# Attention, MoE and gated MLP on one core: weight pieces, x loads and output buffers in the last stage rearranged

## The chip, the cores and the metric

The kernel runs on one core of one Trainium2 chip. The metric is the device time of one execution in microseconds (us), the median of several; lower is better. Every number in this document comes from these times or from the profile of one execution, unless it says otherwise. TensorE is PE in the profile's rows, VectorE DVE, ScalarE ACT, SyncE SP; "SPq" and "ACTq" are the instructions with which SP and ScalarE issue DMAs.

## The reference

Three stages follow one another, in fp32; the two weight-heavy ones, cut to what matters:

```python
S, D, E, F = 576, 512, 8, 1024
attn = softmax(q @ k.T / sqrt(64) + mlp(relative log positions)) @ v
x = attn.transpose(0, 2, 1, 3).reshape(2304, 512)

e_idx = argmax(x @ w_gate, axis=1)
for e in range(8):
    h = maximum(x[mask_e] @ w1[e], 0)
    out[mask_e] = gate * sigmoid_gate * (h @ w2[e])

g = x @ w_gate2
y = (g * sigmoid(g) * (x @ w_val)) @ w_out
```

q, k and v are (4, 8, 576, 64). In the last stage w_gate2 and w_val are (512, 1536) and w_out is (1536, 512); these three lie in DRAM as 64-bit floats, while everything is computed in 32 bits.

## The kernel before

Every fp32 product is made of three products of a high and a low part (hi and lo). A hi part is a ScalarE copy into the matmul type, a lo part a VectorE subtraction of that copy from the value. So each weight that TensorE uses has passed one ScalarE and one VectorE instruction of its own. VectorE and ScalarE work strictly in the order of the program, and so does SP's queue, which issues nearly all DMAs: an instruction that waits holds back what stands behind it.

**Stages.** Attention runs until about 305 us of the span. Then come 64 MoE steps (`h_step`, `y_step`, L582 to L600; 4 batches, 2 halves of the tokens, 8 pieces of the expert), each with 24 products. For each batch one expert is done for all tokens; the tokens of other experts are left to 8 `q_h`/`q_y` steps for one rest expert (L699, L713) and, where these do not do, to a loop (`loop`, L1167). Work beside the steps is hung on step numbers in a list `todo` (`at(n, f)`): after the products of step n, the entries of n are put in the program. Tables such as NS, QL and EC at the top of the file say which step gets what.

**Weight pieces of the last stage.** w_gate2, w_val and w_out are cut into 12 pieces each, 36 in all, numbered 3f + i (f the piece, i which matrix). A piece is 128 x 512 values of 64 bits, 512 KB. `fetch_w` (L969) loads one and `narrow_w` (L977) makes 32-bit floats of it with one ScalarE instruction (`expo`, L984) and three VectorE ones (`b1`, `b2`, `b3`, L987 to L993), where b1 works in place in the raw piece and must not start before `expo` has read it. The hi and lo parts follow (`w_hi`, L1004; `w_lo`, L1007). Three kinds are told apart:

- pieces 0 to 5 ("early", `early_ld`, `early_cv`) are loaded and converted in late MoE steps and kept on chip;
- pieces 6 to 3*NPL - 1, with NPL = 7, are converted during the first NPL steps of the last stage, three in a step (`n_tasks`, L1386), from two raw buffers (`n_load`, L1381): when a piece has been converted, the piece two further on is asked for;
- the 15 pieces from 3*NPL on ("stash", L1016) are converted in the MoE steps of the table NS and written to a DRAM tile `wn` as 32-bit values; later they are read back (`r_load`, L1372).

Pieces of the first two kinds are stored in `wn` too, for use in the other token blocks.

**Last stage.** 36 steps: 3 blocks of 768 tokens (j), 12 pieces (f) each. Function `it(n)` (L1530) writes out step n. TensorE makes g in bank X and the value in bank Y for the two halves of a block, and, in between, the 18 output products of the step before (`outs`, L1503). The first NPL steps of block 0 are "plain": 48 products for X and Y, which need only the weight pieces. The others use sums of quarters of x and of the weights (S1 to S4, made by `x_add`, L1222; the weights' by `w_sums`) in a scheme of seven products (P1 to P7) instead of eight, which takes 42. S1 to S4 get hi and lo parts through `x_hi` (L1228) and `x_lo` (L1235). The extra work of a step is put at letters a to h between the products (`fills`, `x_fill`), and at one letter a VectorE instruction stands ahead of what the step itself needs. In a plain step VectorE's multiply `p_mul` (L1272) reads Y and releases it for the next Y product; there is one for each half, and each stands behind the extra work of its letter (b or f).

x for the sums is loaded by `ld_x` (L1449): for block 0 at the end of step 2 with eight DMAs, and for the next blocks a step after the 7-product steps began. At the end of a block's last step, called pair end here (the sums of the next block are split there, letters c to h of step 11), S1 goes at letter g and S4 at h, and A22 at c of the next step.

**Rest expert.** Its weights are loaded in three parts by `load_w` (L527, the DMAs L533 and L534) into two large rotating buffers of tag "vt", which the raw early pieces use as well (L1030). The table QL gives the steps of the three loads, QC the step of the first conversion (`conv_w`, L539, with L550 on ScalarE and L552 on VectorE).

**End.** In the last step the six output tiles leave through `ot`, three rotating buffers of 512 columns (L1514), copied from PSUM by VectorE (L1524) or ScalarE (L1526) and stored by SP or ScalarE (L1528, L1520, L1521).

Of the kernel before, what the change touches and what calls it, by code (L numbers as in the profile page):

```python
# [37 lines left out]
N0, NPL = 6, 7  # L38
NS = (9, 10, 11, 18, 19, 20, 21, 24, 25, 26, 34, 35, 38, 40, 41)
# [6 lines left out]
QL, QC = ((55, 54, 60), 58)  # L46
# [66 lines left out]
def body(tc, qt, kt, va, vb, ws, moe_w_gate, moe_w_output_gate, moe_w1, moe_w2, w_gate, w_val, w_out, ctab, cst, cst2, out):  # L113
    nc = tc.nc
    with ExitStack() as ctx:
# [900 lines left out]
        def stash(i, n, m):  # L1016

            def cv():
                for f in narrow_w(s_raw(i), s_out(i)):
                    f()  # L1020
                nc.sync.dma_start(wn[n], s_out(i))
            at(m, cv)
# [4 lines left out]
        early = {}  # L1027
# [6 lines left out]
        def early_cv(n):  # L1034
            i, o = divmod(n, 2)
            fs = []
            t = lambda: early[i][:, 2048 + 512 * o:2560 + 512 * o].bitcast(F32)

            def expo():
                if o == 0:  # L1040
                    early["w"] = pers.tile([128, NTOK], F32R, tag=f"xT{i}", name="w0")
                w = early["w"]
                wt.setdefault(n // 3, {})[n % 3] = w[:, 1024 * o:1024 * o + 512], w[:, 1024 * o + 512:1024 * o + 1024]
                fs.extend(narrow_w(early[i][:, 1024 * o:1024 * o + 1024], t()))
                fs[0]()

            def bits():
                for f in fs[1:]:
                    f()
                nc.sync.dma_start(wn[n], t())  # L1050
# [14 lines left out]
        todo = {}  # L1065
# [21 lines left out]
        for i, m in enumerate(NS):  # L1087
            stash(i, 3 * NPL + i, m)
# [61 lines left out]
        for n in range(16 * B):  # L1150
# [12 lines left out]
            if n:  # L1163
                for f in todo.get(n, []):
                    f()
# [190 lines left out]
        with ExitStack() as c2:  # L1356
# [15 lines left out]
            def r_load(f):  # L1372
                if f % 2:
# [59 lines left out]
            def fills(n):  # L1433
# [5 lines left out]
                if 2 <= f < NPL:  # L1439
                    ts = [n_tasks(3 * f + i) for i in range(3)]  # L1440
                    for k, i, js in (("a", 0, (0,)), ("b", 0, (1, 2, 3)), ("c", 0, (4,)), ("c", 1, (0, 1)), ("c", 0, (5,)), ("d", 1, (2, 3)), ("e", 1, (4,)), ("e", 2, (0, 1)), ("e", 1, (5,)),
# [7 lines left out]
            def ld_x(j):  # L1449
                t = xq["xr"] = wp.tile([128, 3072], F32, tag="xr", name="xr").rearrange("p (k h n) -> p k h n", k=4, h=2)  # L1450
                for k in range(4):
                    def row(a, o, w, b, c):
                        nc.sync.dma_start(t[:, k, :, o:o + w], x2[k, :, b, c:c + 2 * w].rearrange("p o (h n) -> p (o h) n", h=2))  # L1453
                    if j == 0:
                        row(0, 0, 256, bass.ds(r0, 1), 0)
                        row(0, 256, 128, bass.ds(r1, 1), 0)
                    elif j == 1:
                        row(0, 0, 128, bass.ds(r1, 1), 256)
                        row(0, 128, 256, bass.ds(r2, 1), 0)
                    else:  # L1460
                        row(0, 128, 256, slice(3, 4), 0)
# [7 lines left out]
            def x_fill(j, i):  # L1469
# [9 lines left out]
                if j and i == 0:  # L1479
                    d["c"] = [lambda: xq["hi"]("A22"), lambda: xq["lo"]("A22")]  # L1480
# [3 lines left out]
                if i == NF - 1 and j < 2:  # L1484
                    for k, v in zip("cdefgh", ("A11", "A12", "S2", "S3", "S1", "S4")):
# [17 lines left out]
            def outs(n, h, m):  # L1503
# [9 lines left out]
                if last:  # L1513
                    o = wp.tile([128, DM], F32, tag="ot", bufs=3, name="ot")  # L1514
                    end = j == 2
                    parts = rows(j, h, m)
# [13 lines left out]
            def it(n):  # L1530
# [19 lines left out]
                if n == N:  # L1550
                    c2_mul(p, nc.vector)
# [81 lines left out]
            n_load(6)  # L1633
            n_load(7)
# [23 lines left out]
```

## Time and profile before

| what | value |
|---|---|
| median of 3 runs | 996.12 us (993.75 to 1000.24) |
| the profiled execution | 996.18 us |
| its span in the trace | 994.3 us |
| its mean granted TensorE clock | 0.991 |
| TensorE busy | 957.6 us, 96% |
| VectorE busy | 690.8 us, 69% |
| ScalarE busy | 528.9 us, 53% |
| share of the chain that ended last | TensorE 35%, VectorE 4%, ScalarE 2%, DMA 2% |

The span is the time from the first to the last event of the trace; the 1.9 us between it and the execution's time lie around it. Busy time leaves out register, branch and semaphore work. The granted clock is what the throttle let TensorE have, as a share of full speed. A bracket behind a row, as [2.06 <-DVE c L1272], is the idle time of that engine ahead of the row and the instruction that ended it. The chain of the last row is a walk back from the last instruction, at each step to what released it.

### The profile page before, as it was taken

The page shows a single profiled execution, that of the slowest core. Times are in us where ns is not written, and L with a number is a line of the kernel's source. Part 1 is how long each engine was busy: PE and PEld are TensorE (multiplying, and loading weights), DVE is VectorE, ACT ScalarE, POOL GpSimd, SP SyncE. Part 2 cuts the span into 40 slices and gives each one's busy share as a digit, 9 for nine tenths or more (in the row PEclk, how much of TensorE's full clock was granted, in tenths as well). Part 3 has the DMA queues.
Part 4 walks back from the last instruction along what each step waited for, and adds up shares of the span by engine and source line. Part 5 has one row for each costly group of instructions (what it writes and reads, how often), then busy time and mean ns, then how long its engine had stood idle before and what let it go on. Part 6 is the DMA issues. An engine that isn't in the chain of part 4 may idle for free. (4 is left out here: it accounts for less than half of the span.)

```text
span 994.3 us, 19678 instructions
## 1 busy us (share of the span) xinstructions
PE 957.6 (96%) x7639; PEld 816.4 (82%) x7639; DVE 690.8 (69%) x1540; ACT 528.9 (53%) x1121; POOL 115.7 (12%) x116
## 2 busy tenths in 40 slices
PE   7979999999999999999998998999999999999997
PEld 2347777777668999999997897899899998999996
DVE  8977788777787477666555566877646677456663
ACT  6777777777775253433434443454534445335542
POOL 2673333343310000000000000000000000000000
PEclk9999999999999999999999999999999999999999
DMA  6785324333044564936745566440122420311111
GB/s 202 206 257 164 117 82 150 96 119 112 2 135 147 172 224 148 343 124 226 237 140 175 169 198 207 145 142 1 53 75 64 127 64 1 128 32 64 64 32 64
DMA packets 88383, 129.47 MB, mean 130 GB/s; under 512 B 13760, under 2 KB 46528, under 8 KB 88288
## 3 DMA queue, kind: packets, MB, share of 16 engines
q1 hardware_dynamic: 87664, 127.28, 39.9%
q8 instruction: 60, 0.98, 0.4%
q10 hardware_dynamic: 624, 0.92, 0.3%
q14 instruction: 35, 0.29, 0.1%
HBM read 92.71 MB, written 35.46 MB: 129 GB/s over the span
## 5 line engine op out<-in xcount | busy, mean ns | idle before, releaser
L271 DVE CUSTOM_DVE_ANT_0 E<-S,bias 128x576 f32<-128x576 f32 x128 | 91.8, 755 | 32.4 <-PE S L267 25.9
L276 ACT ACTIVATE E<-E,st 128x576 f32<-128x576 f32 x144 | 110.4, 769 | 4.3 <-DVE st L271 3.9
L1256 PE MATMUL Y<-fv,ws 128*128 128x384 f32 x522 | 105.4, 336 | 0.2
L1256 PEld LDWEIGHTS Y<-fv,ws 128*128 128x128 f32 x522 | 92.4, 188 | 3.8 <-DVE c L1281 0.7
L267 PEld LDWEIGHTS S<-kh,qz 64*128 64x128 f32 (+1 forms) x576 | 57.7, 189 | 38.5 <-DVE st L271 21.0
L378 PE MATMUL pv<-pt,rawv 128*64 128x320 f32 (+1 forms) x576 | 88.1, 422 | 0.0
L267 PE MATMUL S<-kh,qz 64*128 64x288 f32 (+1 forms) x576 | 84.0, 325 | 3.9 <-DVE st L271 2.6
L1512 PE MATMUL o<-ws,u 128*128 128x512 f32 x306 | 84.5, 395 | 1.2 <-DVE u L1311 1.2
L591 ACT ACTIVATE qz<-T 128x288 fp32r<-128x288 f32 x63 | 25.8, 409 | 89.5 <-PE T L589 89.3
L317 ACT ACTIVATE pt<-T 128x512 f32<-128x512 f32 (+3 forms) x112 | 50.7, 468 | 40.4 <-PE T L294 40.0
L1256 PE MATMUL X<-fr,ws 128*128 128x384 f32 x348 | 70.9, 338 | 0.0
L1007 DVE TENSOR_TENSOR ws<-r,ws 128x512 fp32r<-128x512 f32 (+1 forms) x63 | 49.1, 779 | 30.3 <-ACT ws L1004 29.5
L1256 PEld LDWEIGHTS X<-fr,ws 128*128 128x128 f32 x348 | 62.8, 188 | 5.5
L1512 PEld LDWEIGHTS o<-ws,u 128*128 128x128 f32 x306 | 56.2, 188 | 8.7 <-DVE u L1311 2.5
L602 PE MATMUL y<-qz,w2hl 128*128 128x288 f32 x384 | 57.0, 296 | 2.1 <-DVE qz L592 0.8
L319 DVE COPY pt<-T 128x512 f32<-128x512 f32 (+3 forms) x112 | 55.8, 522 | 3.3 <-PE T L294 3.1
L592 DVE SCALAR_TENSOR_TENSOR qz<-T,qz 128x288 fp32r<-128x288 f32 x63 | 28.7, 455 | 41.4 <-ACT qz L591 40.8
L589 PE MATMUL T<-xh,whl 128*128 128x288 f32 x256 | 56.9, 298 | 0.0
L602 PE MATMUL y<-qz,whl 128*128 128x288 f32 x384 | 56.7, 296 | 0.1
L589 PE MATMUL T<-xh,w1hl 128*128 128x288 f32 x248 | 55.7, 300 | 0.0
L602 PEld LDWEIGHTS y<-qz,w2hl 128*128 128x128 f32 x384 | 52.7, 188 | 3.5 <-ACT qz L591 2.3
L294 PE MATMUL T<-ident,E 64*128 64x64 f32 x1248 | 55.3, 224 | 0.0
(308 smaller groups left out, 2136.7 us busy)
## 6 DMA issues: line engine op xcount, KB each, us to landing
raww<-in_moe_w_dram SPq DMA_DIRECT2D x16, 768.0 KB, 6.7
r<-wn SPq DMA_DIRECT2D x21, 512.0 KB, 3.6
bscr<-ob SPq DMA_DIRECT2D x36, 288.0 KB, 3.6
bias<-bscr SPq DMA_DIRECT2D x14, 576.0 KB, 4.3
ro<-wn SPq DMA_DIRECT2D x21, 256.0 KB, 2.8
rawq<-in_qt_dram SPq DMA_DIRECT2D x16, 320.0 KB, 3.6
rawk<-in_kt_dram SPq DMA_DIRECT2D x16, 288.0 KB, 3.2
x<-xT SPq DMA_DIRECT2D x16, 288.0 KB, 6.3
```

What stands on the lines that cost most here:

```text
L267: nc.tensor.matmul(t[:, f, 0:288], x[k, a], y[k, o], start=i == 0, stop=i == 2)
L271: nc.vector.tensor_tensor_reduce(out=E.rearrange("p (a b) -> p a b", a=2), in0=ps[:, :, 0:288], in1=bt[p, hh, c].rearrange("p (a b) -> p a ...
L276: nc.scalar.activation(E, E, AF.Exp, bias=st[:, 2 * c + hh:2 * c + hh + 1], scale=-1.0, accum_out=st[:, 10 + 2 * c + hh:11 + 2 * c + hh])
L294: nc.tensor.transpose(t[r][:, at:at + 64], E[k, o:o + 128], ident[k, k])
L317: nc.scalar.activation(o, x, AF.Copy)
L319: nc.vector.tensor_copy(o, x)
L378: nc.tensor.matmul(st["ps"][64 * hh:64 * hh + 64, 0:w], vt[p][:, hh, b, c, :], y, start=c == order[0], stop=c == order[4])
L589: nc.tensor.matmul(ps, wa[:, x, k], xs[k][y][:, o], start=k == 0 and i == 0, stop=k == 3 and i == 2)
L602: nc.tensor.matmul(hbuf["y"][d // 2][:, d % 2, 0:288], wb[:, x, d], t[:, y:y + 288], start=f == 0 and i == 0, stop=(one or f == 7) and i == 2)
L1007: return lambda: eng.tensor_tensor(l, t, h.bitcast(F32), ALU.subtract)
L1256: nc.tensor.matmul(bank, a[:, c], x[:, k], start=first and k == 0 and n == 0, stop=k == 1 and n == 2, skip_group_check=True)
L1512: nc.tensor.matmul(t, u, w, start=first and i == 0, stop=last and i == 2)
```

## The change

It has seven parts, and the line numbers of the changed file lie 1 to 21 higher.

1. NPL goes from 7 to 6. One plain step becomes a 7-product step, and its three pieces (18 to 20) join the stash: NS has 18 entries at partly other steps, and four of them (NS2) leave the last instruction of the conversion to the next step.
2. The stores of stashed and early pieces into `wn` are hung on a second list `done` (`after(n, f)`), whose entries come behind all of `todo` in a step, and one to two steps later than before.
3. The rest expert's loads move from steps 55, 54, 60 to 58, 55, 61 (QL).
4. Raw pieces are fetched three ahead instead of two: every third takes a tile of the tag r0. In the plain steps the exponent of a piece (`expo`) is put ahead of the hi part of the piece before it.
5. x for the blocks 0 and 1 is loaded with four DMAs instead of eight, and for block 2 with ten instead of twelve. With NPL = 6, S1 and S2 are made in step 3 and S3 and S4 in step 4 (before 4 and 5), while the load stays at the end of step 2.
6. At the pair ends S1 moves from letter g to h, S4 from h to c of the next step, and A22 from c to d there.
7. The last step's output goes through one tile `oend` of six slices in the place of x (tag xr).

The diff, cut to its core:

```diff
-N0, NPL = 6, 7
-NS = (9, 10, 11, 18, 19, 20, 21, 24, 25, 26, 34, 35, 38, 40, 41)
+N0, NPL = 6, 6
+NS = (9, 10, 13, 18, 19, 20, 21, 24, 25, 26, 29, 34, 35, 37, 39, 40, 41, 43)
+NS2 = (13, 29, 37, 43)
-QL, QC = ((55, 54, 60), 58)
+QL, QC = ((58, 55, 61), 58)
-        def stash(i, n, m):
+        def stash(i, n, m, two):
...
-                for f in narrow_w(s_raw(i), s_out(i)):
-                    f()
-                nc.sync.dma_start(wn[n], s_out(i))
-            at(m, cv)
+            at(m, lambda: cv(0, 4 if not two else 3))
+            if two:
+                at(m + 1, lambda: cv(3, 4))
+            after(m + 1 + two, lambda: nc.sync.dma_start(wn[n], s_out(i)))
...
+            after((52, 52, 54, 54, 57, 57)[n], lambda: nc.sync.dma_start(wn[n], t()))
...
-                for f in todo.get(n, []):
+                for f in todo.get(n, []) + done.get(n, []):
                     f()
...
-                    nw[n] = wp.tile([128, 1024], I32, tag="nraw", bufs=2, name="nraw")
+                    if n % 3 < 2:
+                        nw[n] = wp.tile([128, 1024], I32, tag="nraw", bufs=2, name="nraw")
+                    else:
+                        nw[n] = wp.tile([128, 2048], F32, tag="r0", name="nr2").bitcast(I32)[:, 0:1024]
...
-                    n_load(n + 2)
+                    n_load(n + 3)
...
+                def row(o, w, b, c):
+                    for h in range(2):
+                        nc.sync.dma_start(t[:, :, h, o:o + w], x2[:, :, b, c + h * w:c + h * w + w].rearrange("k p o n -> p k (o n)"))
+                if j == 0:
+                    row(0, 256, bass.ds(r0, 1), 0)
+                    row(256, 128, bass.ds(r1, 1), 0)
...
                 if j and i == 0:
-                    d["c"] = [lambda: xq["hi"]("A22"), lambda: xq["lo"]("A22")]
+                    for k, v in zip("cd", ("S4", "A22")):
+                        d[k] = [lambda v=v: xq["hi"](v), lambda v=v: xq["lo"](v)]
...
-                    for k, v in zip("cdefgh", ("A11", "A12", "S2", "S3", "S1", "S4")):
+                    for k, v in zip("cdefh", ("A11", "A12", "S2", "S3", "S1")):
...
-                    o = wp.tile([128, DM], F32, tag="ot", bufs=3, name="ot")
                     end = j == 2
+                    if end:
+                        o = sv["end"][:, 512 * (3 * h + m):512 * (3 * h + m) + 512]
+                    else:
+                        o = wp.tile([128, DM], F32, tag="ot", bufs=3, name="ot")
```

**Where instructions move: SP's queue at the end of the MoE.** The names: raww are the rest expert's weights, rw0 the raw early pieces with their 32-bit values, qz00 a tile of x. Before:

```order
L533 DMA raww_7322<-in_moe_w1_dram 128x4x384
L534 ISA
L534 DMA raww_7322<-in_moe_w2_dram 128x3x512
L759 ISA
L759 DMA qz00_114<-x2_120 128x4x256
L533 ISA
L533 DMA raww_7360<-in_moe_w1_dram 128x4x384
L534 ISA
L534 DMA raww_7360<-in_moe_w2_dram 128x3x512
L1050 DMA wn_4870<-rw0_7252 128x512 x2
L533 ISA
L533 DMA raww_7542<-in_moe_w1_dram 128x4x256
```

And of the change:

```order
L760 DMA qz00_114<-x2_120 128x4x256
L534 ISA
L534 DMA raww_7375<-in_moe_w1_dram 128x4x384
L535 ISA
L535 DMA raww_7375<-in_moe_w2_dram 128x3x512
L1067 DMA wn_4870<-rw0_7270 128x512 x2
L534 ISA
L534 DMA raww_7492<-in_moe_w1_dram 128x4x384
L535 ISA
L535 DMA raww_7492<-in_moe_w2_dram 128x3x512
L534 ISA
L534 DMA raww_7593<-in_moe_w1_dram 128x4x256
```

The store of the last early pair stood behind the second request for raww and stands ahead of it now; that request takes another buffer than before (the program's numbers behind the names tell buffers' uses apart, not the buffers).

**ScalarE in the second plain step.** tw are 32-bit pieces, nraw and nr2 raw ones, ws the hi parts, c1 and c2 results from bank X. Before:

```order
L984 ACTIVATE tw_8098<-nraw_8089 128x512
L1268 ACTIVATE c1_8095<-X_8093 128x384
L1308 ACTIVATE u00_8085<-c1_8095 128x384
L1004 ACTIVATE ws_8097<-tw_8098 128x512
L984 ACTIVATE tw_8138<-nraw_8091 128x512
L1268 ACTIVATE c2_8096<-X_8093 128x384
L1004 ACTIVATE ws_8097<-tw_8138 128x512
L984 ACTIVATE tw_8170<-nraw_8117 128x512
L1308 ACTIVATE u10_8087<-c2_8096 128x384
L1004 ACTIVATE ws_8097<-tw_8170 128x512
```

And of the change:

```order
L985 ACTIVATE tw_8118<-nraw_8107 128x512
L1279 ACTIVATE c1_8115<-X_8113 128x384
L1319 ACTIVATE u00_8103<-c1_8115 128x384
L985 ACTIVATE tw_8157<-nraw_8109 128x512
L1005 ACTIVATE ws_8117<-tw_8118 128x512
L1279 ACTIVATE c2_8116<-X_8113 128x384
L985 ACTIVATE tw_8189<-nr2_8111 128x512
L1005 ACTIVATE ws_8117<-tw_8157 128x512
L1319 ACTIVATE u10_8105<-c2_8116 128x384
L1005 ACTIVATE ws_8117<-tw_8189 128x512
```

The exponent of the second piece (tw from nraw) stood behind the hi part of the first and now stands ahead of it, and likewise for the third, which comes from nr2.

**VectorE in the fourth plain step (step 3), of the change.** sx are the sums of x, xr is x, nraw a raw piece, Y the bank:

```order
L1008 TENSOR_TENSOR ws_8232<-tw_8301,ws_8232 128x512
L1322 TENSOR_TENSOR fv_7968<-c2_8231,fv_7967 128x384
L988 TENSOR_SCALAR nraw_8252<-nraw_8252 128x512
L991 SCALAR_TENSOR_TENSOR tw_8349<-tw_8349,nraw_8252 128x512
L994 SCALAR_TENSOR_TENSOR tw_8349<-nraw_8252,tw_8349 128x512
L1233 TENSOR_TENSOR sx_8342<-xr_8337 128x768
L1283 TENSOR_TENSOR c1_8345<-Y_8344,c1_8345 128x384
```

The sixth row is S1. In the same step of the kernel before nothing stands there: the multiply of Y and c1 comes right behind the three instructions of the piece, and S1 follows one step later.

## Rows read from the trace of the kernel before

**Rows 1.** Page part 1, whole span: busy time of each engine, share, instructions.

```profile
PE 957.6 (96%) x7639; PEld 816.4 (82%) x7639; DVE 690.8 (69%) x1540; ACT 528.9 (53%) x1121; POOL 115.7 (12%) x116
```

**Rows 2.** Stretches of the span: columns as told in the prediction.

```profile
core 0: us, PE busy (x) PEld busy (x) DVE busy (x) ACT busy (x) POOL busy (x), PEclk, DMA share, GB/s
...
588.32:600.87 12.55, 12.55 (x68) 11.75 (x67) 8.39 (x15) 4.71 (x9) 0.00 (x0) 1.00 0.92 300
600.87:614.97 14.10, 12.76 (x68) 11.65 (x67) 9.80 (x17) 4.67 (x10) 0.00 (x0) 1.00 0.52 162
614.97:631.38 16.41, 14.35 (x67) 12.97 (x66) 11.06 (x20) 6.41 (x12) 0.00 (x0) 0.90 0.62 208
631.38:644.64 13.26, 12.77 (x67) 11.66 (x66) 11.59 (x20) 6.82 (x12) 0.00 (x0) 1.00 0.25 80
691.24:702.80 11.56, 11.56 (x62) 10.75 (x60) 6.82 (x11) 6.71 (x12) 0.00 (x0) 1.00 0.00 0
702.80:715.55 12.75, 12.12 (x61) 10.64 (x60) 8.62 (x15) 6.09 (x12) 0.00 (x0) 1.00 0.17 62
842.70:855.40 12.70, 12.05 (x62) 10.57 (x61) 8.66 (x15) 6.04 (x12) 0.00 (x0) 1.00 0.18 66
534.00:536.00 2.00, 2.00 (x16) 2.00 (x17) 1.62 (x5) 0.83 (x4) 0.00 (x0) 1.00 0.52 171
621.00:623.00 2.00, 2.00 (x9) 2.00 (x8) 1.97 (x4) 0.87 (x2) 0.00 (x0) 0.63 0.99 349
623.00:625.00 2.00, 2.00 (x6) 1.52 (x6) 1.97 (x4) 0.00 (x0) 0.00 (x0) 0.52 0.73 279
```

**Rows 3.** Timeline of TensorE, plain steps: start, us, engine, line, tile, idle before.

```profile
605.16 2.32 PE L1265 MATMUL Y<-fv,ws 128*128 128x384 f32 x12 [1.34 <-DVE c L1272]
...
619.99 2.93 PE L1265 MATMUL Y<-fv,ws 128*128 128x384 f32 x12 [2.06 <-DVE c L1272]
```

**Rows 4.** Timeline of VectorE, plain steps: the multiplies that release bank Y.

```profile
590.05 0.55 DVE L1272 TENSOR_TENSOR c<-Y,c 128x384 f32<-128x384 f32 x1
...
604.47 0.55 DVE L1272 TENSOR_TENSOR c<-Y,c 128x384 f32<-128x384 f32 x1
...
609.87 0.55 DVE L1272 TENSOR_TENSOR c<-Y,c 128x384 f32<-128x384 f32 x1
...
619.29 0.55 DVE L1272 TENSOR_TENSOR c<-Y,c 128x384 f32<-128x384 f32 x1
```

**Rows 5.** Timelines of SP's queue and of ScalarE, plain steps.

```profile
591.23 4.78 SPq L1453 DMA_DIRECT2D xr<-x  x8
...
601.48 0.68 ACT L984 ACTIVATE tw<-nraw 128x512 f32<-128x512 f32 x1 [1.19 <-DMA nraw<-in_w_out_dram]
```

**Rows 6.** Timelines of SP, VectorE, ScalarE, TensorE: the rest expert's weights.

```profile
525.12 0.37 SPq L533 DMA_DIRECT2D raww<-in_moe_w_dram  x1
...
518.61 0.69 DVE L1007 TENSOR_TENSOR w<-rw,w 128x512 fp32r<-128x512 f32 x1 [0.33 <-ACT w L1004]
...
524.40 0.69 DVE L552 TENSOR_TENSOR w2hl<-raww,w2hl 128x512 fp32r<-128x512 f32 x1
...
529.99 0.63 ACT L550 ACTIVATE w1hl<-raww 128x512 fp32r<-128x512 f32 x1 [3.56 <-DMA raww<-in_moe_w_dram]
...
534.00 0.38 PE L704 MATMUL T<-qx,whl 128*128 128x256 f32 x1 [2.43 <-DVE qz L592]
```

**Rows 7.** Timelines of VectorE and TensorE, the first pair end.

```profile
703.14 0.96 DVE L1235 TENSOR_TENSOR fr<-sx,fr 128x768 fp32r<-128x768 f32 x1 [1.33 <-ACT fr L1228]
...
705.09 0.50 PE L1512 MATMUL o<-ws,u 128*128 128x512 f32 x1 [0.60 <-DVE u L1311]
```

**Rows 8.** Timeline of all engines, last 12 us of the span.

```profile
988.14 0.69 DVE L1524 COPY ot<-o 128x512 f32<-128x512 f32 x1 [2.13 <-DMA out_dram<-ot]
...
991.32 0.36 ACTq L1521 DMA_DIRECT2D out_dram<-ot  x1
```

**Rows 9.** Timeline of TensorE in the MoE.

```profile
348.29 0.40 PE L602 MATMUL y<-qz,w2hl 128*128 128x288 f32 x1 [0.75 <-ACT qz L591]
```

More of the change, by code (lines that the diff above doesn't have):

```diff
@@ L1014, in s_out, with cv, fs, after @@
             return xT[2][:, 512 * (i % 2):512 * (i % 2) + 512]
-        def stash(i, n, m):
-            def cv():
-                for f in narrow_w(s_raw(i), s_out(i)):
-                    f()
-                nc.sync.dma_start(wn[n], s_out(i))
-            at(m, cv)
+        def stash(i, n, m, two):
+            def cv(k, e):
+                for f in fs()[k:e]:
+                    f()
+            fl = []
+            def fs():
+                if not fl:
+                    fl.extend(narrow_w(s_raw(i), s_out(i)))
+                return fl
+            at(m, lambda: cv(0, 4 if not two else 3))
+            if two:
+                at(m + 1, lambda: cv(3, 4))
+            after(m + 1 + two, lambda: nc.sync.dma_start(wn[n], s_out(i)))
         def stash_ld(i, n, m):
             at(m - 3, lambda: fetch_w(n, s_raw(i)))
-        early = {}
+        early, todo, done = {}, {}, {}
+        def after(n, *fs):
+            done.setdefault(n, []).extend(fs)
         def early_ld(i):
@@ L1049, in bits @@
                     f()
-                nc.sync.dma_start(wn[n], t())
             def halves():
@@ L1064, in pvs @@
                     pvq.pop(0)()
-        todo = {}
         def at(n, *fs):
@@ L1087, in body @@
         for i, m in enumerate(NS):
-            stash(i, 3 * NPL + i, m)
+            stash(i, 3 * NPL + i, m, m in NS2)
         for i, m in enumerate(NS):
@@ L1372, in r_load @@
             def r_load(f):
-                if f % 2:
+                if f % 2 == NPL % 2:
                     rr[f] = pers.tile([128, NTOK], F32, tag="xT2", name="r1")
@@ L1440, in fills @@
                     ts = [n_tasks(3 * f + i) for i in range(3)]
-                    for k, i, js in (("a", 0, (0,)), ("b", 0, (1, 2, 3)), ("c", 0, (4,)), ("c", 1, (0, 1)), ("c", 0, (5,)), ("d", 1, (2, 3)), ("e", 1, (4,)), ("e", 2, (0, 1)), ("e", 1, (5,)),
+                    for k, i, js in (("a", 0, (0,)), ("b", 0, (1, 2, 3)), ("c", 1, (0,)), ("c", 0, (4,)), ("c", 1, (1,)), ("c", 0, (5,)), ("d", 1, (2, 3)), ("e", 2, (0,)), ("e", 1, (4,)), ("e", 2, (1,)), ("e", 1, (5,)),
                                      ("f", 2, (2, 3)), ("g", 2, (4, 5))):
@@ L1450, in ld_x @@
                 t = xq["xr"] = wp.tile([128, 3072], F32, tag="xr", name="xr").rearrange("p (k h n) -> p k h n", k=4, h=2)
[L1451 to L1461, printed above, removed]
+                def row(o, w, b, c):
[4 more added lines that the diff above has]
+                    row(256, 128, bass.ds(r1, 1), 0)
+                elif j == 1:
+                    row(0, 128, bass.ds(r1, 1), 256)
+                    row(128, 256, bass.ds(r2, 1), 0)
+                else:
+                    row(128, 256, slice(3, 4), 0)
+                    for k in range(4):
                         for h in range(2):
@@ L1513, in outs @@
                 if last:
-                    o = wp.tile([128, DM], F32, tag="ot", bufs=3, name="ot")
                     end = j == 2
+                    if end:
+                        o = sv["end"][:, 512 * (3 * h + m):512 * (3 * h + m) + 512]
+                    else:
+                        o = wp.tile([128, DM], F32, tag="ot", bufs=3, name="ot")
                     parts = rows(j, h, m)
@@ L1550, in it @@
                 if n == N:
+                    sv["end"] = wp.tile([128, 3072], F32, tag="xr", name="oend")
                     c2_mul(p, nc.vector)
@@ L1631, in it @@
                     ld_x(j + 1)
-            n_load(6)
-            n_load(7)
+            for n in range(6, 9):
+                n_load(n)
             for n in range(1, len(steps) + 1):
```

## Prediction

> **What bounds the kernel now.** I read the page's busy table first. TensorE works 957.6 us, 96% of the span [rows 1], so in the kernel as it stands only TensorE's idle time, its products and the end behind it can give anything. The view of TensorE's waits named three places, and tables of stretches (us, then busy time by engine, granted clock, DMA share, GB/s) size them.
>
> First, the plain steps of the last stage, each 48 products of 8 per piece. Undisturbed, one takes 12.55 us and a 7-product step 11.56; the three plain steps from 600.87 take 14.10, 16.41 and 13.26 [rows 2]. They exceed 12.55 by 1.55 + 3.86 + 0.71 = 6.12 us. TensorE's timeline shows why: bank Y isn't read in time, 1.34 us before 605.16 and 2.06 us before 619.99 [rows 3]. Behind the second wait the clock is between its levels of 2.4 and 1.2 GHz, 0.63 and 0.52 of full speed over two stretches of 2 us [rows 2], so 2 x 0.37 + 2 x 0.48 = 1.7 us of that 6.12 is clock.
>
> VectorE reads Y late because it runs in order and is behind. Its multiply that releases Y (L1272) stands at 590.05 in a step that met no x, then 604.47, then 619.29 [rows 4], so a pair of multiplies takes 14.4 to 14.8 us in place of 12.55. One cause is that the eight transfers of x hold SP's queue for 4.78 us from 591.23, and the next raw piece is asked for behind them: ScalarE starts that piece at 601.48 after waiting for its DMA [rows 5]. The other is in each piece: VectorE cannot begin the bit work until ScalarE has written the exponent, and ScalarE does that last.
>
> Second, the rest expert's weights: SP asks for the second third only at 525.12, after VectorE's last use of the buffer that it takes over (524.40, 0.69 us), ScalarE waits 3.56 us for it until 529.99, and TensorE stands 2.43 us before 534.00 [rows 6]. Third, the two pair ends: the steps at 702.80 and 842.70 take 12.75 and 12.70 [rows 2]. The end behind the last product is the fourth item.
>
> **The change, part by part.**
>
> *Rest weights.* The second third now takes a buffer of an early raw pair. Its last user on VectorE is the subtraction at 518.61 (0.69 us, so 519.3) [rows 6]; the store of that pair, now right ahead on SP, must land too, and 1.1 us for that is my estimate. Request 520.4 instead of 525.12: 4.7 us earlier, more than the 3.56 us that ScalarE waits. The third third is no longer held either. TensorE's 2.43 us then go: gain 2.4. Bounds: 0 if the store is late in the queue and the wait returns, 2.43 if all goes; I take the upper, since 4.7 exceeds 3.56 by over a microsecond.
>
> *Plain steps.* One of them becomes a 7-product step: 12.55 - 11.56 = 0.99 us [rows 2], its three pieces moving to the MoE. For the rest I walk VectorE's chain. With the exponent made one piece ahead, VectorE loses two waits a step, each as long as an exponent (0.68 us at 601.48; I take 0.65) [rows 5], so the multiply of 590.05 is bound by TensorE's Y alone, about 588.2. SP goes on as before: x was asked for 1.18 us after that multiply (591.23 against 590.05) [rows 4, 5], so now from 589.4, in four issues at about 0.6 us (4.78 us for eight). Ahead of it stands one raw piece of 0.5 MB; x has 1.57 MB. In the step of 588.32 DMA moved 300 GB/s at a share of 0.92 [rows 2], which is 326 at full share: 2.07 MB / 326 = 6.4 us, begun at about 589, with 0.8 us to start and to be seen: x is there at 596.2. At 300 GB/s and slower starts it is 597.5; at 349 GB/s, which the row of 621 shows [rows 2], 595.0.
>
> The Trainium skill ("DMA: Bandwidth & Descriptors", Anatomy of one DMA — SWDGE) fits a transfer as some 2.0 us fixed plus its bytes at 436 GB/s. An estimate by that, for a queue that it did not measure, has x there at about 595.6, and the sum 0.6 us better; the row's 300 GB/s at a share of 0.92 lies below its rate, and no run here shows 436, so I keep the row's.
>
> Now the added wait. The first sum S1 reads x and stands one step earlier, ahead of the multiply that was at 594.58. All of VectorE waits with it till 596.2; the multiply follows at 597.1 (S1 takes 0.9). That is still in time for Y. The next multiply came 9.42 us after this kind (609.87 to 619.29, one sum included) [rows 4]; less 1.3 for the two waits, 8.1: 605.2. TensorE's Y begins 0.69 after that multiply (605.16 after 604.47), at 605.9, and wants it at 603.7 (605.16 less its 1.34 wait, less 0.1 of overlap): a stall of about 2.2. The following pair of multiplies takes 14.8 (604.47 to 619.29) less 1.3 = 13.5: 618.7, so Y at 619.4. TensorE, 2.2 late, wants it at 618.45 (603.7 + 12.55 + 2.2): a second stall of 0.95. For the clock I put half of 1.7, since the 1.34 us wait left it at 1.00 in its step (row of 600.87) and so did the 2.43 us wait (row of 534), while the 2.06 us wait did not [rows 2, 3, 6].
>
> The Trainium skill ("TensorE: Matmul & The Clock Gate", What's actually happening) has the gate go by how busy the engine was of late, between two levels. By that a stall of 2.2 us may or may not cost; the rows above agree, as the longer wait was the free one. Taken as always or never, the sum moves 0.85 either way.
>
> Together 2.2 + 0.95 + 0.85 = 4.0 against 6.12: 2.1 us, and 0.99 for the changed step: 3.1. Bounds: x later by 1.3 takes 1.3 and the other half of the clock, leaving 0.9; x at 595.0 or sooner, no clock loss, 5.2; with no stall left, 7.1.
>
> *Pair ends.* ScalarE and VectorE split S1 there between two instructions that TensorE waits for: VectorE's 703.14 waits 1.33 us for ScalarE, and TensorE 0.60 before 705.09 [rows 7]. S1 now goes behind them and S4 into the next step, where products on A11 and A12 come first and cover them. The steps then take 11.56: 1.19 + 1.14 = 2.3. Bounds: 1.2, twice the 0.60, if the waits that follow it stay, and 2.3. I take 2.3; if the cover fails, S4 is late at its product in the next step and some of it returns.
>
> *Tail.* The last outputs wait for an old buffer's DMA: VectorE 2.13 us before 988.14, and ScalarE's last DMA goes out at 991.32 [rows 8]. With six slices nothing waits, and ScalarE's own chain of copies and issues ends the work at about 989.7: gain 1.6. Bounds 0.6 (if the DMAs, not the buffers, pace it) and 2.1.
>
> *MoE.* Three more pieces are converted there, each one ScalarE and three VectorE instructions of at most the 0.69 us of a full 128x512 one [rows 6], so 8.3 us of work beside TensorE, over three of 64 steps. Stores now stand behind loads. I put this at nothing: the page's shares of VectorE and ScalarE, 69% and 53% [rows 1], are the cover, and where it is gone TensorE waits for an eviction. TensorE stood 0.75 us before 348.29, where a weight was late [rows 9]; such stalls could go (gain 0.75) or appear at several of the 18 places (0.75 each). Bounds -1 to +4 us. The later blocks' x, in four transfers, has whole 7-product steps as cover.
>
> **Sum.** 2.4 + 3.1 + 2.3 + 1.6 = 9.4 us. The profiled execution took 996.18 (span 994.3 and 1.9 around it), 0.06 above the median of the runs shown, so 996.2 - 9.4 = **986.8**, 0.9% less. A measurement of this kernel tells about 1% from no change.
>
> **Rivals.**
> 1. *VectorE catches up entirely.* x lands at 594.5 or before, no stall is left in the plain steps (7.1 instead of 3.1), and the stall at 348 goes: 996.2 - 9.4 - 4.0 - 0.75 = 982.0; half way 984. For it: raw pieces now lie three ahead and the wait on ScalarE goes. Against: 2.07 MB cannot land so soon at the rates shown. Chance 0.28.
> 2. *The MoE pays.* Three more conversions and the new places push VectorE past its step at five places at 0.75 us, 3.75: 990.6. Against: fifteen such pieces cost almost nothing before. Chance 0.20.
> 3. *The rest weights wait as before.* The store ahead of them is late on SP, so the change does not do what it says there: 2.4 less, 989.2. Chance 0.06.
> 4. *Stores stuck behind loads, slower.* A stash's output slice is used again two pieces later, at the shortest two steps later, and its store is now issued behind the loads of the step after. Where such a load waits for its buffer, as at 525.12, the store does too, ScalarE's exponent for the later piece waits in its order, and the MoE's own evictions queue behind it. A place costs what the rest weights cost, 2.43 and half the clock's 1.7, together 3.3 us. From the third place on the gain of 9.4 is spent: 996.2 - 9.4 + 9.9 = 996.7; more places, above 1006. Against: most loads there go out without a wait. Chance 0.06.
> 5. *The forecast itself,* within about 2 us of 986.8. Chance 0.40.
>
> **How the numbers follow.** Faster by over 1% means below 986.2. The forecast lies 0.6 above that: of its 0.40 I give 0.16 to faster, with nearly all of rival 1, so 0.43. Within 1% hold the rest of the forecast and rivals 2 and 3, together with most of rival 4: 0.52. Slower by over 1% only the worst of rival 4: 0.05. The range runs from rival 1 with no stall left, 981.8, to rival 2 with a stall to spare, 992.0; what lies outside is rival 4 and little else. The forecast's own range is 984.8 to 988.8.
>
> **What would show it.** In the profile after: TensorE without a wait at the rest expert's first products; ScalarE's exponents (L985) without their wait for DMA; VectorE waiting for x once, ahead of S1, until about 596 (some 2.4 us earlier on the new time line); two stalls on Y, near 2.2 and 1; 11.56 us for both pair ends; no wait on an output buffer in the last 10 us. I would be wrong if x lands more than 1.5 us off, if ScalarE shows waits for stores of pieces in the MoE, or if the step behind a pair end waits for S4.

## The result, and the profile after

The changed kernel takes 1005.4 us (median of 7 runs, 1002.27 to 1007.01) against 996.12 (993.73 to 1000.24): ratio 1.009, with a 95% interval of 1.0067 to 1.0113. It is slower by 0.9%, where 986.8 us and 0.9% faster were forecast, and it lies outside the stated range. The profiled execution took 1007.01 us, at the upper end, with a span of 1005.1.

The page's clock row shows at once that something happened in the MoE. It is the clock granted in 40 slices of 25 us, first in the kernel before and then in this one:

```profile
PEclk9999999999999999999999999999999999999999
...
PEclk9998999999999999798999999999999999999999
```

The seventeenth and nineteenth slice (402 to 427 and 452 to 477 us) stand at 0.7 and 0.8, where before had 0.9 and more throughout; the 0.8 of the fourth lies in attention. TensorE's waits over the whole span (us in total, times, longest) name what happened there:

```profile
PE rps L516 <- DVE rl L509: 7.0, 1, 7.0
PE y L603 <- ACT qz L592: 6.1, 2, 5.1
```

Before, the first row wasn't there, and the second was this:

```profile
PE y L602 <- ACT qz L591: 0.7, 1, 0.7
```

In the list of ScalarE's waits in the MoE a releaser appears that the kernel before did not have at all, the store of a stashed piece; its timeline shows the two large ones of the three, and TensorE's timeline what they cost:

```profile
ACT xT L985 <- DMA wn<-xT: 18.0, 3, 9.0
```

```profile
408.39 0.66 ACT L985 ACTIVATE xT<-xT 128x512 f32<-128x512 f32 x1 [9.02 <-DMA wn<-xT]
...
469.29 0.66 ACT L985 ACTIVATE xT<-xT 128x512 f32<-128x512 f32 x1 [8.13 <-DMA wn<-xT]
...
410.44 0.61 PE L603 MATMUL y<-qz,w2hl 128*128 128x288 f32 x1 [5.14 <-ACT qz L592]
412.59 3.01 PE L603 MATMUL y<-qz,w2hl 128*128 128x288 f32 x11 [1.55 <-DVE qz L593]
...
472.73 0.26 PE L516 MATMUL rps<-rl,cst_sb 32*1 32x32 f32 x2 [6.96 <-DVE rl L509]
```

The exponent of the piece of step 26 starts at 408.39 after 9.02 us of waiting for a store, that of step 41 at 469.29 after 8.13. ScalarE's eviction for the MoE stands behind it, so TensorE is idle for 5.14 + 1.55 us at the first place and 6.96 at the second. Behind each the clock falls to half (us, busy time of PE, PEld, DVE, ACT and POOL with counts, clock, DMA share, GB/s; the first row is from ahead of the first place):

```profile
400.00:404.00 4.00, 4.00 (x32) 4.00 (x32) 0.00 (x0) 0.00 (x0) 0.00 (x0) 1.00 1.06 387
...
412.00:416.00 4.00, 3.41 (x14) 3.41 (x15) 3.31 (x7) 0.76 (x2) 0.00 (x0) 0.50 0.92 346
...
472.00:476.00 4.00, 3.27 (x22) 3.22 (x23) 2.57 (x12) 0.00 (x0) 0.00 (x0) 0.50 0.25 92
```

Why the store is late, SP's and VectorE's timelines show:

```profile
393.65 0.69 DVE L994 SCALAR_TENSOR_TENSOR xT<-xT,xT 128x512 int32<-128x512 int32 x1
...
396.38 0.41 SPq L534 DMA_DIRECT2D raww<-in_moe_w_dram  x1
396.98 0.39 SPq L535 DMA_DIRECT2D raww<-in_moe_w_dram  x1
397.60 0.37 SPq L534 DMA_DIRECT2D raww<-in_moe_w_dram  x1
398.19 0.84 SPq L535 DMA_DIRECT2D raww<-in_moe_w_dram  x1
399.44 0.34 SPq L1031 DMA_DIRECT2D wn<-xT  x1
```

VectorE has finished the piece of step 24 at 394.34 (393.65 + 0.69). Its store goes out at 399.44 only, 5.1 us later, since SP works in order and four loads of expert weights (768 KB each) stand ahead of it. They wait for the number of the expert, so the first goes out 2.0 us behind the finished piece (396.38), and issuing the four takes the other 3.1. Once issued the store takes 8.9 us to land, while DMA moves 387 GB/s at a share of 1.06 (row of 400 above): 3 MB of weights and 0.5 MB of a raw piece are in flight with it. The next row is the view of DMA issues for this one store, with size and time to landing:

```profile
wn<-xT SPq DMA_DIRECT2D x1, 256.0 KB, 8.9
```

The piece of step 26 takes the output slice of the piece of step 24, so its exponent must wait until that store has landed. At the second place the store of step 39 went out at 460.22, among the last expert's weights, and took 9.0 us.

In the kernel before a stash store landed in 2.2 us in the median. The store of step 24 went out ahead of the weights there (first row, landed in 2.0 us). The median hides that a store among the same loads was slow in that kernel too: the one of step 26 went out at 399.89 and landed in 8.1 us (second row). Nobody waited for it, since its slice was not written again before step 35.

```profile
392.38 0.33 SPq L1021 DMA_DIRECT2D wn<-xT  x1
...
wn<-xT SPq DMA_DIRECT2D x1, 256.0 KB, 8.1
```

How much each part cost or gave can be read by laying the starts of the same ScalarE evictions (L591 before, L592 after) and TensorE products of both traces side by side:

| from, to | before | after | after minus before | its change |
|---|---|---|---|---|
| first eviction of the MoE | 302.59 | 304.61 | 2.0 | +2.0 (attention) |
| behind the first place | 413.59 | 425.05 | 11.5 | +9.5 |
| ahead of the second place | 449.09 | 460.74 | 11.7 | +0.2 |
| behind the second place | 466.21 | 486.51 | 20.3 | +8.6 |
| ahead of the rest expert | 526.02 | 546.07 | 20.1 | -0.2 |
| behind the rest expert's first products (TensorE) | 534.97 | 552.38 | 17.4 | -2.6 |
| last T products ahead of the loop (TensorE) | 546.32 | 563.27 | 17.0 | -0.5 |
| third plain step (step 2) | 575.77 | 591.46 | 15.7 | -1.3 |
| end of the first 7-product steps | 656.58 | 670.84 | 14.3 | -1.4 |
| behind the second pair end | 855.40 | 867.25 | 11.9 | -2.4 |
| last DMA issue | 991.32 | 1001.92 | 10.6 | -1.3 |

The 2.0 us of attention are not the change's: over the kernels of this study, which leave attention alone, the first eviction lies between 300.7 and 304.6. The MoE costs 18.1 us up to the rest expert. What stands behind it gives 2.6 + 0.5 + 1.3 + 1.4 + 2.4 + 1.3 = 9.5, of which the first 1.3, at the loop, is not the change's either, as told below.

The lines that answer to [rows 6]: SP's request for the second third of the rest expert's weights, ScalarE's first conversions of it, the first without a wait (before 3.56 us) and the second with 1.21, and the rest expert's first product, without one (before 2.43):

```profile
541.44 0.39 SPq L534 DMA_DIRECT2D raww<-in_moe_w_dram  x1
...
546.38 0.62 ACT L551 ACTIVATE w1hl<-raww 128x512 fp32r<-128x512 f32 x1
548.21 0.63 ACT L551 ACTIVATE w2hl<-raww 128x512 fp32r<-128x512 f32 x1 [1.21 <-DMA raww<-in_moe_w_dram]
...
550.59 0.28 PE L705 MATMUL T<-qx,w1hl 128*128 128x256 f32 x1
```

The request of 541.44 is 521.4 on the time line of before (less the 20.05 us of the table): 3.7 us ahead of 525.12.

The plain steps that answer to [rows 2 to 5]: stretches first (columns as above), then SP, VectorE and TensorE:

```profile
604.00:618.48 14.48, 12.85 (x68) 11.70 (x67) 6.58 (x13) 4.64 (x9) 0.00 (x0) 1.00 0.74 241
618.48:635.08 16.60, 14.18 (x67) 13.07 (x66) 13.38 (x23) 5.91 (x11) 0.00 (x0) 0.90 0.53 175
635.08:647.63 12.55, 12.55 (x68) 11.76 (x66) 10.88 (x19) 6.82 (x12) 0.00 (x0) 1.00 0.30 87
...
601.75 0.43 SPq L974 DMA_DIRECT2D nraw<-in_w_val_dram  x1
...
605.15 2.70 SPq L1468 DMA_DIRECT2D xr<-x  x4
...
614.08 0.96 DVE L1233 TENSOR_TENSOR sx<-xr 128x768 f32<-128x768 f32 x1 [5.48 <-DMA xr<-x]
614.96 0.55 DVE L1283 TENSOR_TENSOR c<-Y,c 128x384 f32<-128x384 f32 x1
...
623.16 0.55 DVE L1283 TENSOR_TENSOR c<-Y,c 128x384 f32<-128x384 f32 x1
...
636.77 0.55 DVE L1283 TENSOR_TENSOR c<-Y,c 128x384 f32<-128x384 f32 x1
...
615.56 2.38 PE L1276 MATMUL Y<-fv,ws 128*128 128x384 f32 x12 [1.63 <-DVE c L1283]
...
623.86 3.71 PE L1276 MATMUL Y<-fv,ws 128*128 128x384 f32 x12 [2.42 <-DVE c L1283]
```

VectorE waits 5.48 us for x and makes S1 at 614.08, 8.9 us after the request. Two stalls follow, 1.63 and 2.42 us, and low clock: the two steps exceed 12.55 by 1.93 + 4.05 = 5.98 us, nearly the 6.12 of before. For a pair of multiplies VectorE needs 13.6 us (623.16 to 636.77), where it needed 14.8.

The two pair ends [rows 2, 7], and the end [rows 8]:

```profile
717.05:728.61 11.56, 11.56 (x62) 10.75 (x60) 8.13 (x15) 6.72 (x12) 0.00 (x0) 1.00 0.23 85
855.70:867.25 11.55, 11.55 (x62) 10.75 (x60) 8.12 (x15) 6.72 (x12) 0.00 (x0) 1.00 0.22 81
...
994.34 4.50 PE L1529 MATMUL o<-ws,u 128*128 128x512 f32 x18
...
1001.92 0.36 ACTq L1541 DMA_DIRECT2D out_dram<-oend  x1
```

Both steps take 11.56 and 11.55 (before 12.75 and 12.70). From the last products' start to the last DMA issue it is 7.58 us; before it was 8.87 (982.45 to 991.32).

### The profile page after: what moved, and what is told of

The parts are those of the page before. It is cut to its first block, busy times and chain, and to the rows that moved or that the text cites. A ratio compares the mean times of both kernels' runs of the same rounds, so it can differ in the third digit from the quotient of the medians.

```text
span 1005.1 us, 19647 instructions
## 1 busy us (share of the span) xinstructions
PE 959.9 (96%) x7633; PEld 819.7 (82%) x7633; DVE 694.7 (69%) x1548; ACT 531.3 (53%) x1125; POOL 115.8 (12%) x116
## 5 line engine op out<-in xcount | busy, mean ns | idle before, releaser
L1267 PE MATMUL Y<-fv,ws 128*128 128x384 f32 x540 | 108.8, 336 | 0.0
L1267 PEld LDWEIGHTS Y<-fv,ws 128*128 128x128 f32 x540 | 95.7, 188 | 3.0 <-issue 0.2
L592 ACT ACTIVATE qz<-T 128x288 fp32r<-128x288 f32 x63 | 25.8, 409 | 94.7 <-PE T L590 94.5
L1008 DVE TENSOR_TENSOR ws<-r,ws 128x512 fp32r<-128x512 f32 (+1 forms) x66 | 51.4, 779 | 31.9 <-ACT ws L1005 30.9
L1267 PE MATMUL X<-fr,ws 128*128 128x384 f32 x360 | 73.4, 339 | 0.0
L1267 PEld LDWEIGHTS X<-fr,ws 128*128 128x128 f32 x360 | 65.0, 188 | 5.6
```

What stands on the lines that cost most here:

```text
L1008: return lambda: eng.tensor_tensor(l, t, h.bitcast(F32), ALU.subtract)
L1267: nc.tensor.matmul(bank, a[:, c], x[:, k], start=first and k == 0 and n == 0, stop=k == 1 and n == 2, skip_group_check=True)
```

## The experiments

Theory A: in the MoE, ScalarE's exponent waits for the store of the piece two before, and that store is late because it was put behind the loads of the expert's weights. Rivals: the three more pieces and their new steps (B); late raw loads (C). All times below are medians; each ratio is to the kernel before on the same chip.

**Stores back.** The edit in the changed kernel:

```diff
-            after(m + 1 + two, lambda: nc.sync.dma_start(wn[n], s_out(i)))
+            at(m + two, lambda: nc.sync.dma_start(wn[n], s_out(i)))
```

> The changed kernel with the stores of the stashed pieces back in the step of their conversion, ahead of that step's and the next step's loads; all else as changed. Theory A (in the MoE, ScalarE's exponent waits for the store of the piece two before, whose output slice it takes, and that store shares the DMA engines with the expert's weights asked for ahead of it): the waits of 9.02 and 8.13 us on ScalarE vanish, the 9.5 and 8.7 us that the two places cost in the profile go, and the time is 1005.4 - 18 = 987.4. Rival B (the three more pieces and their new steps load the DMA engines and ScalarE there, wherever the stores stand): at least one of the two waits of TensorE stays, over 995. Rival C (the stores' place costs nothing, the pieces' raw loads are what is late): no change, 1005.

988.49 us (ratio 0.9923, 0.9903 to 0.9943). One line accounts for 17 us of difference to the changed kernel. In its trace the exponent of step 26 waits for nothing, but ScalarE now waits for the last expert's weights:

```profile
394.69 0.67 ACT L985 ACTIVATE xT<-xT 128x512 f32<-128x512 f32 x1
...
454.91 0.63 ACT L551 ACTIVATE w1hl<-raww 128x512 fp32r<-128x512 f32 x1 [4.26 <-DMA raww<-in_moe_w_dram]
```

There the evictions fall back by 2.2 us against those of before, the one thing in which the change's table costs something once the stores are back.

**Only the stores moved.** In the kernel before:

```diff
-                nc.sync.dma_start(wn[n], s_out(i))
             at(m, cv)
+            done.setdefault(m + 1, []).append(lambda: nc.sync.dma_start(wn[n], s_out(i)))
...
-                for f in todo.get(n, []):
+                for f in todo.get(n, []) + done.get(n, []):
```

> The kernel before with only the stores of the stashed pieces moved, behind all other work of the step after their conversion; its 15 pieces keep their steps. Theory A: the steps 24, 25, 26 are the same in both kernels, so that place appears here too, and costs its 9.5 us: 1005.6. The second place needs pieces two steps apart in the same slice behind the weights of the last expert (39 and 41), and before has 38, 40, 41: a third less distance is missing, so it stays away or is small. Rivals B and C: within 1% of 996, no wait of ScalarE for a store.

1010.06 us (1.0137, 1.0117 to 1.0157): slower than the change itself. The place of step 26 is there, and a further one that was not expected:

```profile
351.48 0.66 ACT L984 ACTIVATE xT<-xT 128x512 f32<-128x512 f32 x1 [3.90 <-issue]
...
411.20 0.66 ACT L984 ACTIVATE xT<-xT 128x512 f32<-128x512 f32 x1 [9.03 <-DMA wn<-xT]
```

The kernel before has pieces at steps 9, 10, 11, the change at 9, 10, 13. So here the exponent of step 11 meets the store of step 9. Its wait of 3.90 us has no releaser in the profile ("issue"), but that store went out at 342.47 and took 8.9 us to land, until 351.4, where the exponent starts. The evictions fall back by 3.6 us there and by 9.4 at step 26. The change's table had already made room at one of three places. Rivals B and C fall: no piece was added, and no raw load moved.

**A third output slice.** In the changed kernel, stores left late:

```diff
-            return xT[2][:, 512 * (i % 2):512 * (i % 2) + 512]
+            j = i % 2 if i < 10 else 0 if i % 3 == 0 else 1 if i % 3 == 1 else 2
+            o = (0, 512, 1152)[j]
+            return xT[2][:, o:o + 512]
```

> The changed kernel with the stores where the change put them, but a third output slice for the pieces from step 29 on, so that a slice comes up again three pieces later; the pieces before step 29 keep two. Theory A: the second place (exponent of step 41, before 8.13 us of waiting) vanishes and the first (9.02 us, step 26) stays: 1005.4 - 8.7 = 996.7. Rival B or C: both stay, 1005.

996.33 us (1.0004, 0.9987 to 1.002). The exponent of step 26 (first row) still waits, that of step 41 (second) no longer does, with the store of step 39 where it was, between the weights:

```profile
404.37 0.66 ACT L985 ACTIVATE xT<-xT 128x512 f32<-128x512 f32 x1 [8.98 <-DMA wn<-xT]
...
455.66 0.66 ACT L985 ACTIVATE xT<-xT 128x512 f32<-128x512 f32 x1
...
463.35 0.66 ACT L985 ACTIVATE xT<-xT 128x512 f32<-128x512 f32 x1
```

The store of step 39 goes out at 454.90 and still takes 8.2 us to land; the next exponent that takes its slice is now that of step 43 (third row), and it waits for nothing. So it is the slice that the exponent waits for, and the late store alone costs nothing there.

**x a step earlier.** In the kernel with the stores back:

```diff
-                    if i == 2:
+                    if i == 1:
                         ld_x(0)
```

> Kernel e1 with the x of the last stage's first block asked for one plain step earlier (end of step 1 instead of step 2). Theory A with this: the first sum finds x there (VectorE waited 5.48 us for it in the changed kernel), the waits of 1.63 and 2.42 us on bank Y and the low clock behind them, together 6.0 us over undisturbed steps, shrink to about 1.5: 987.4 - 4.5 = 982.9. Rival: x takes the DMA engines from the raw pieces of step 2 and 3, ScalarE's exponents wait instead, and the gain is under 1.5 us: 986 or more.

982.31 us (0.9857, 0.9837 to 0.9878). S1 waits for nothing, and the plain steps 3 and 4, which have the sums, are undisturbed:

```profile
592.22 0.95 DVE L1233 TENSOR_TENSOR sx<-xr 128x768 f32<-128x768 f32 x1
...
587.70:600.24 12.54, 12.54 (x67) 11.75 (x66) 9.69 (x18) 5.39 (x10) 0.00 (x0) 1.00 0.58 188
600.24:612.79 12.55, 12.55 (x68) 11.75 (x66) 9.74 (x18) 5.20 (x10) 0.00 (x0) 1.00 0.55 192
```

The gain is 6.2 us on the kernel with the stores back, more than the 4.5 expected: no stall is left at all.

**Rest weights alone, ends alone.** The kernel before with QL and the early pieces' stores of the change; the kernel before with `x_fill` and `oend` of the change:

> The kernel before with only the rest expert's loads at their new steps and the early pieces' stores at their new ones. The forecast's term: TensorE's 2.43 us at the rest expert's first products go, 996.2 - 2.4 = 993.8. What the changed kernel's trace suggests instead: evictions of the MoE there come 3.6 us earlier against those of before, 992.6. Rival (in the changed kernel the place only gained because the MoE ahead of it was late and the weights had time): no gain, 996.

> The kernel before with only the pair ends' splits moved and the six output slices at the end. The forecast's terms: 2.3 + 1.6 = 3.9, so 992.3, with steps of 11.56 us at both pair ends and no wait for an output buffer. Rival (S4 is late in the next step, the outputs are paced by their DMAs): under 2 us, 994.5 or more.

993.15 us (0.9964, 0.9949 to 0.998) and 993.01 us (0.995, 0.9931 to 0.9969). In the first, TensorE's wait ahead of the rest expert's products is 0.15 us instead of 2.43; in the second the step of the first pair end takes 11.55:

```profile
531.16 0.39 PE L704 MATMUL T<-qx,whl 128*128 128x256 f32 x1 [0.15 <-DVE qz L592]
```

```profile
700.22:711.77 11.55, 11.55 (x62) 10.75 (x60) 8.12 (x15) 6.72 (x12) 0.00 (x0) 1.00 0.20 73
```

Both rivals fall: by the medians (996.87 for the kernel before) the parts give 3.7 and 3.9 us (by the intervals 2.0 to 5.1 and 3.1 to 6.9), without a late MoE ahead.

**Stores at the end of their own step**, with x early:

```diff
-            at(m + two, lambda: nc.sync.dma_start(wn[n], s_out(i)))
+            after(m + two, lambda: nc.sync.dma_start(wn[n], s_out(i)))
```

> Kernel e4 (x a step earlier) with the stashed pieces' stores at the end of the conversion's own step, so behind that step's loads but ahead of the next step's. Theory A, refined (a store issued behind one third of the weights, 1.5 MB, still shares the DMA engines with the third after it): at step 26 ScalarE waits for a store again, but for 2 to 4 us instead of 9, and TensorE for 0 to 2 us: 982.3 to 985. Rival (only the issue order counts, and one step earlier is enough): no wait for a store anywhere, 982.3, or better by the 2 us that weights behind stores cost at step 43.

987.03 us (0.9896, 0.9861 to 0.993), by the medians, of two chips, 4.7 more than with the store ahead of the step's loads, and more than expected:

```profile
395.56 0.41 SPq L1031 DMA_DIRECT2D wn<-xT  x1
...
402.48 0.67 ACT L985 ACTIVATE xT<-xT 128x512 f32<-128x512 f32 x1 [5.02 <-DMA wn<-xT]
```

The store goes out between the two thirds, 1.1 us behind the first load's request (394.46) where it was 3.1 in the changed kernel, but is in flight with both and takes 6.9 us to land; the exponent waits 5.02 us. Evictions fall back by 4.2 us there. A store needs not stand behind all loads to be late: one third ahead of it and one behind were enough here.

**The exponent's order**, with x early, put back; the entries of letter c are shown:

```diff
-("c", 1, (0,)), ("c", 0, (4,)), ("c", 1, (1,)), ("c", 0, (5,)),
+("c", 0, (4,)), ("c", 1, (0, 1)), ("c", 0, (5,)),
```

Letter e is changed likewise.

> Kernel e4 with the exponents in the plain steps back behind the hi part of the piece before, as before the change; raw pieces still three ahead, x still early. Theory A for the plain steps (VectorE's chain of two multiplies took 14.8 with the two waits for an exponent and 13.6 without): with x there in time the chain with sums is still over 12.55, so each step with sums adds 1.3: waits on bank Y come back, 2 to 3 us in all, 984.5 to 985.5. Rival (with x early the slack hides the exponents): 982.3.

987.51 us (0.989, 0.9856 to 0.9925): by the medians, of two chips, 5 us slower than with the exponent ahead, where 2 to 3 were expected. Both stalls are back, 4.0 us in all, and the chain of two multiplies takes 14.83 us again (589.35 to 604.18):

```profile
604.88 2.32 PE L1276 MATMUL Y<-fv,ws 128*128 128x384 f32 x12 [1.95 <-DVE c L1283]
...
619.71 2.32 PE L1276 MATMUL Y<-fv,ws 128*128 128x384 f32 x12 [2.06 <-DVE c L1283]
```

**Three attempts at the 2.2 us of the last expert's weights**, all with x early, and the kernel with x early once more for comparison:

> Kernel e4 once more, on the chip of the two below, for their comparison: 982.3.

> Kernel e4 with the table of the stash from step 34 on at steps 34, 35, 36, 37, 45, 46, 47 instead of 34, 35, 37, 39, 40, 41, 43, so that no raw piece is fetched at steps 35 to 41 and none is stored at 38 to 44, around the last expert's weights. Theory (a raw piece asked for right ahead of the weights makes them 0.5 MB later, ScalarE waits 3.6 to 4.3 us for them and TensorE loses 2.2 us there): the loss goes, 982.3 - 2.2 = 980.1. Rival (the later steps are full: steps 45 to 47 have the rest expert's bookkeeping, and pieces there make VectorE late): 982 to 985.

> Kernel e4 with the table's end as in the kernel before (34, 35, 38, 40, 41) and the other two pieces at 31 and 45. Same theory: the weights of step 40 and 41 stand behind no raw piece, 980.1. Rival (any third-batch weights wait with three more pieces on the queue): 982.3.

> Three parts of the runs so far in one kernel: stashed pieces before step 29 stored in their own step, those from step 29 on stored behind the loads as in the changed kernel but with three output slices, and x asked for one plain step earlier. Theory (behind the loads a store costs nothing once nobody waits for its slice, and the last expert's weights then come earlier: in the kernel with three slices ScalarE waited only 0.70 and 1.82 us for them): no wait for a store, none of the 2.2 us at the last expert's weights, 982.5 - 2.2 = 980.3. Rival (the two parts undo each other, the store's place before step 29 moves the wait elsewhere): 982.5 or more.

982.81 us (0.987, 0.9852 to 0.9889), 981.36 (0.9859, 0.9838 to 0.988), 984.74 (0.9886, 0.9855 to 0.9917) and, in a comparison of its own, 983.26 (0.985, 0.9826 to 0.9875). At the weights all three do what was expected: laid beside before, the evictions no longer fall back by 2 us there. In the time it can't be seen. Further on something comes back, 1.6 us by the 52nd of 63 evictions in the first, 2.8 in the second and 0.8 in the mixed kernel (0.8 in the kernel with x early itself). What it is was not found. Inconclusive as a gain: the four intervals overlap, and none of them is told apart from the kernel with x early. Each of the four beats both kernels.

Not tested apart: raw pieces three ahead, x in four transfers, and one plain step less.

## Why the prediction was wrong

**The step that failed** is the last of the parts, "MoE. ... I put this at nothing", with its bounds of -1 to +4 us. It measured +18.1 us in the profile, and 17 us went in the run that only put the stores back. The cover that I named, the shares of VectorE and ScalarE, was the wrong question: neither was short of time. I didn't follow the moved DMA to the buffer that it releases. The edit puts a store behind other transfers; its slice is written again two pieces later; so the wait to look for was ScalarE's for that slice. Two of the signs of being wrong that I had named came: waits for stores of pieces in the MoE, and x over 1.5 us off.

**Rival 4** had this dependency, with a chance of 0.06. Two of its numbers were wrong. It had the store held by loads that wait for a buffer, and argued "most loads there go out without a wait". They need not wait for one: 5.1 us pass in the queue, 2.0 until the expert is known and 3.1 while the loads are issued, and 8.9 more in flight with 3.5 MB, although [rows 2] showed that DMA moves 300 to 349 GB/s when busy. 3.5 MB at that rate are 10 to 12 us, against 6.4 us for two MoE steps (evictions 3.19 us apart): that sum was open to me and spoke for a wait at steps 24, 25, 26, as did the store that took 8.1 us to land in the trace of before. At steps 18 to 21, as close together but with no weights asked for, the waits came to 0.9 us in all. And it priced a place at 3.3 us; the two measured 9.5 and 8.6.

**The other terms** were nearly right one by one, but for the plain steps. They come to 8.2 us, where 9.4 were forecast:

- Rest weights: forecast 2.4. By TensorE's own starts they measured 2.6 at the first products and 0.5 behind them; in the run with this part alone 2.3 at the first products, and 3.7 by the medians (996.87 there against 993.15). TensorE's wait went as described, but not for the whole of the reason: the request came 3.7 us earlier instead of 4.7, and ScalarE kept a wait of 1.21 us, and of 2.94 in the run with this part alone. No run shows the 1.1 us that I had put for the store; in that run the pair's second store took 3.7 us to land.
- Plain steps: forecast 3.1, measured 1.4. The chain was right: 8.2 us from the first multiply to the next (forecast 8.1), 13.6 for the pair (13.5). Wrong was x: forecast 6.8 us after its request, measured 8.9. The rate was right; in the trace DMA moves about 320 GB/s between 604 and 614 us. I had counted one raw piece ahead of x; there was another in flight, asked for at 601.75, and two stores. No run shows the 0.8 us to start and to be seen by itself, and by the same sum the bound for 349 GB/s is 595.7, not 595.0. So the multiply after S1 was late for its own Y as well (1.63 us ahead of 615.56), where I had it in time, and the 2.42 us stall ran into half clock. With x a step earlier no stall was left, and with the exponents put back two stalls returned: the 6 us go only with both.
- The loop: 1.3 us in the table that were not in the forecast and are not the change's. TensorE waited 1.65 us there in both kernels; behind it the clock was 0.50 in the kernel before and 1.00 in the changed one. The run with the ends alone has the loop of the kernel before and the same wait, but the clock stayed at 1.00 and the same 1.3 us were gained. So the 9.5 us of the table meet the 9.4 of the forecast by chance.
- Pair ends: forecast 2.3, measured 2.4 (1.2 each).
- Tail: forecast 1.6, measured 1.3.

With the stores back the changed kernel takes 988.5; less the 2.2 us that its table costs at the last expert's weights, which I had not foreseen, that is 986.3, by the forecast of 986.8. Part of that is luck, since the plain steps gave 1.7 us less than forecast and the rest weights 0.7 more. The plan of the change holds, but for one line and for x, which comes too late.

## What to carry to other kernels

When a DMA is moved back in a queue, ask who waits for it to land, not only who waits for the queue: a store frees a buffer, and the time to the buffer's next use has to cover the queue ahead of it and all bytes that are in flight with it. Look up the landing of the one transfer that will be waited for; the median of its kind can hide it. A third buffer made the same late store free, and where there is no room for one, the store belongs ahead of the large loads. Put a load whose data an in-order engine meets first, as x here, a whole step earlier before changing anything behind it: count every transfer that is still in flight, not only the one ahead.

## What was not expected of the hardware

- A 256 KB store in flight with 3.5 MB of loads took 8.9 us, against a median of 2.2 us in the kernel before, where two such stores took 8.1 and 8.6 us as well. It landed at 408.3, behind the three of the four weight loads ahead of it whose landing the trace has (4.8, 6.3 and 8.1 us after their issue). In the kernel with stores at the end of their own step, a store issued between two weight loads (395.56) still held the next exponent until 402.48.
- TensorE waited 1.65 us at the loop in both kernels and in the run with the ends alone. The granted clock then was 0.50 over the next 2 us in the kernel before (first row) and 1.00 in the changed one (566 to 570) and in that run (second row). Neither the length of the wait nor the kernel's text decided it.

```profile
550.00:552.00 2.00, 2.00 (x5) 1.53 (x5) 1.62 (x4) 1.48 (x4) 0.00 (x0) 0.50 0.69 160
...
547.00:549.00 2.00, 1.75 (x8) 1.27 (x8) 1.12 (x3) 1.78 (x5) 0.00 (x0) 1.00 0.50 145
```

- Attention, the same in all kernels, ended up to 3.9 us apart between executions (first eviction of the MoE at 300.7 to 304.6), which is the size of most terms here. At the first expert's weights (eleventh to twelfth eviction) two executions of one kernel, with x early, gained 0.2 and 1.6 us on the kernel before. Terms were therefore read from stretches within one trace.
